# Sampled values of the fifth query group: twelve block transfers from SP's queue in place of four gathers from GpSimd

## The chip, the cores and the metric

The kernel runs on one core of a Trainium2 chip. The metric is the device time of one execution in microseconds (us). The core's engines run side by side and wait for each other by semaphores: PE (TensorE) multiplies and transposes, DVE (VectorE), ACT (ScalarE) and POOL (GpSimd) work on tiles, and SP (SyncE) only issues transfers. SP issues a transfer by itself, in the order of its queue. A gather by a list of rows is issued on POOL, as an instruction between POOL's other work.

## The reference, cut to what matters

```python
# attention: batch 4, 8 heads, 768 positions, head width 64; blocks of 32 positions
scores = scale * np.matmul(q, k.transpose(0, 1, 3, 2))
mask = np.abs(blk_i - blk_j) <= 1                      # the window of three blocks
mask = mask | (blk_i == 0) | (blk_j == 0) | (blk_i == n_blocks - 1) | (blk_j == n_blocks - 1)
for qb in range(n_blocks):
    for kb in sampled_blocks[qb]:                      # three sampled blocks for each query block
        mask[qb * block:(qb + 1) * block, kb * block:(kb + 1) * block] = True
attn = softmax(np.where(mask, scores, -1e9))           # then out = attn @ v
# mixture of experts on the 3072 rows of 512: each token goes to one of 8 experts, 384 tokens each,
# by the descending order of all logits x @ w_gate
for e in range(E):
    mask = assigned == e
    out[mask] = np.maximum(x[mask] @ w1[e], 0.0) @ w2[e]
```

## The kernel before, in words

**Two stages.** `Attn` computes the attention of the four batches one after the other, writes its rows to HBM (`xrows`) and the gate's logits to a tile (`lg`). `Moe` then orders the tokens expert by expert, gathers 384 rows for each expert, multiplies them with weights that were split in two halves, and scatters the results to the output.

**Attention.** A batch's 24 query blocks of 32 positions make one dense part (the first and the last block, kind `D`) and six groups `u` of four blocks each (the sixth, `u` = 5, has two). A query block of a group sees eight key blocks. Four stand in the tile `kg` ahead of the sampled ones (the window of three, and the first or last block), and in the value tile `vw`; the three sampled blocks and the last block stand in the value tile `vz`. `kg` and `vw` have two buffers (`u % 2`), `vz` has three (`u % 3`). For each pair of halves PE multiplies keys and queries (L482), DVE subtracts the row's extreme (L524, L529), PE transposes (L550), ACT takes the exponential (L556), and PE multiplies with the values of `vw` and of `vz` in turn (L577, the value products).

**The sampled values.** `values` writes a batch's value rows with a one behind each head's 64 values (520 words a row, 2080 bytes) to HBM, `vrows`, one tensor for each batch. `group_values` then fills `vz[32 * r : 32 * r + 32, g]` for each query block g and sampled block r, in one of two ways. Where `u` is odd, SP reads the block numbers of the group into registers (L393) and issues a transfer of 32 rows for each block, three for each query block (L397). Where `u` is even, POOL issues one gather of 96 rows for each query block, by the list `vidx` (L401).

**What sets the order.** The instructions of the attention are tasks of a planner (`Plan`). Each task has a place in time, engines on which it may run with a duration for each, and what it needs; the planner takes the tasks one by one, gives copies that may run on either of two engines to the one that ends earlier by its numbers, and writes the instructions out in the order that comes of it. A gather counts 1.22 us of POOL, three transfers 1.6 us of SP. What changes in one task may so move others. The order of `Moe` is made by another clock (`Clock`), which starts at zero and knows nothing of the attention.

**The end.** In the last expert the results leave in three parts j. Ahead of each scatter POOL writes a one-word spacer, and ahead of the first of the three it also issues a transfer `words` of 34 separate words of each of 128 partitions, from a constant tile to a tile that nothing reads.

Of the kernel before, what the change touches and what calls it, by code (L numbers as in the profile page):

```python
# [7 lines left out]
F32 = mybir.dt.float32  # L8
# [167 lines left out]


NG = 2


class Attn:
# [151 lines left out]
    def group_keys(self, b, u, n):  # L333
# [9 lines left out]
        def add(eng, fn):  # L343
            t = pl.add(n, eng, fn, deps=ev + [self.base], after=ts[:1], take=[s] if first[0] else [],
                       use=[s, self.Tslot[b]["k"]], row="kg" if first[0] else None)
            first[0] = False
            ts.append(t)
        any_ = lambda p, a: dict(POOL=p, ACT=a)
        if u < 2:
            for o, t in ((96, 0), (224, S - BS)):  # L350
                def f(e, o=o, t=t):
                    self.copy(e, kg()[:, :, :, o:o + BS], kT()[:, :, None, t:t + BS].to_broadcast([128, HP, 4, BS]))
                add(any_(.6, .7), f)

        for g in range(0, len(self.blocks(u)), NG):
            def f(e, g=g):
                k = kT()
                a = [list(d) for d in k.ap]
                src = bass.AP(tensor=k.tensor, offset=k.offset + 128 * u + BS * g, ap=a[:2] + [[BS, NG], [1, 96]])
                self.copy(e, kg()[:, :, g:g + NG, 0:96], src)  # L360
            add(any_(.4 + NG * .32, .16 + NG * .33), f)

# [12 lines left out]
    def group_values(self, b, u, n):  # L375

        nc, pl = self.nc, self.plan
        vw, vz, vn = self.vw[u % 2], self.vz[u % 3], self.vn[b % 2].rearrange("p c h d -> p c (h d)")
        sw, sz, sn = pl.slot("vw"), pl.slot("vz"), self.vnslot[b]
        self.vslot[b, u] = [sw, sz]  # L380
        ld, bl, tw, tz = self.vld[b], self.blocks(u), [], []

        def aw(eng, fn, need=(), move=0.0, late=0.0):
            tw.append(pl.add(n + late, eng, fn, deps=[ld[c] for c in need] + [self.base], after=tw[:1],
                             take=[] if tw else [sw], use=[sw, sn], move=move, row=None if tw else "vw"))

        def az(eng, fn, deps, move=0.0, late=0.0):
            tz.append(pl.add(n + late, eng, fn, deps=deps, after=tz[:1], take=[] if tz else [sz], use=[sz, sn], move=move, row=None if tz else "vz"))
        both = lambda p, a: dict(POOL=p, ACT=a)
        for g in range(len(bl)) if u % 2 else ():  # L390
            def f(g=g):
                if u not in self.kept:
                    self.kept[u] = nc.values_load_multi_w_load_instructions(  # L393
                        self.tz[0:1, bl[0]:bl[-1] + 1].rearrange("p n r -> p (n r)"), engines=[ET.SP], min_val=0, max_val=NB,
                        skip_runtime_bounds_check_because="the table is clamped on the chip")[1]
                for r in range(3):
                    nc.sync.dma_start(vz[32 * r:32 * r + 32, g], self.vs[b][bass.ds(self.kept[u][3 * g + r] * BS, BS)])  # L397
            az(("SP", 1.6 if b or g else 3.2), f, self.rel[b] + [self.idx], move=0.75, late=0.1 * g)
        for g in range(len(bl)) if u % 2 == 0 else ():
            def f(g=g):  # L400
                nc.gpsimd.indirect_dma_start(out=vz[0:96, g], out_offset=None, in_=self.vs[b],  # L401
                                             in_offset=bass.IndirectOffsetOnAxis(ap=self.vidx[:, bl[g]:bl[g] + 1], axis=0))
            az(("POOL", 1.22), f, self.rel[b] + [self.idx], move=0.8, late=0.1 * g)
        if u < 3:
            def f():
                nc.sync.dma_start(vz[96:128], vn[96:128, 5:6].to_broadcast([32, 4, VR]))
            az(("SP", 0.5), f, [ld[5]], move=0.75)
        if u < 2:
            def f():
                nc.sync.dma_start(vw[96:128], vn[0:32, 0:1].to_broadcast([32, 4, VR]))  # L410
            aw(("SP", 0.5), f, [0], move=0.75)
        for g in range(len(bl)):
            c = [(bl[g] + i) // 4 for i in (-1, 0, 1)]
            q = [32 * ((bl[g] + i) % 4) for i in (-1, 0, 1)]
            at = [(i, 1) for i in range(3)]
            if g == 0 and u:
                at = [(0, 3)]
            elif g == 2:
                at = [(0, 2), (2, 1)]
            for i, w in at:  # L420
                if bl[g] + i - 1 in (0, NB - 1):
                    def f(g=g, i=i):
                        nc.gpsimd.memset(vw[32 * i:32 * i + 32, g], 0.0)
                    aw(("POOL", 0.53), f)
                    continue

                def f(e, g=g, i=i, w=w, c=c[i], q=q[i]):
                    self.copy(e, vw[32 * i:32 * (i + w), g], vn[q:q + 32 * w, c])
                aw(both(.62, .64), f, [c[i]])
        self.vt[b, u] = tw + tz  # L430
# [389 lines left out]
class Moe:  # L820
# [349 lines left out]
    def ffn(self, k):  # L1170
        nc = self.nc
        xh, xl = self.x[k]
        hh = self.xp.tile([128, 8, CAP], F32R, name="hh", bufs=1)
        hl = self.xp.tile([128, 8, CAP], F32R, name="hl", bufs=1)
        lows, ps = [], {}

        def first(f, passes):
            wh, wl = self.weights(8 * k + f // 2)
            o = 128 * (f % 2)
            if 0 in passes:  # L1180
                ps[f] = self.acc()
            for n in passes:
                a, b = ((wh, xh), (wl, xh), (wh, xl))[n]
                for d in range(4):
                    if n == 2:
                        self.force(self.xlow[k][d])
                    self.P.matmul(ps[f], a[:, 256 * d + o:256 * d + o + 128], b[:, d],
                                  start=n == 0 and d == 0, stop=n == 2 and d == 3)
                    yield

        def relu(f):
            self.A.activation(hh[:, f], ps[f], AF.Relu)
            lows.append(self.add(self.low(hl[:, f], ps[f], hh[:, f], OP.max), "DVE", [hh[:, f]], LOW))
            self.open.append(lows[-1])
            if f % 2:
                self.conv(8 * k + f // 2 + LEAD + (2 if k == E - 1 else 0))

        if k == 0:
            yield from first(0, (0, 1))
            yield from first(1, (0, 1))  # L1200
        for f in range(8):
            yield from first(f, (2,) if k == 0 and f < 2 else (0, 1, 2))
            relu(f)
        po = [self.p1.tile([128, DM], F32, name=f"po{j}") for j in range(3)]
        self.second[k] = True

        def product(f, j):
            wh, wl = self.weights(8 * k + 4 + f // 2)
            o = 512 * (f % 2)
            for n, (a, b) in enumerate(((hh, wh), (hl, wh), (hh, wl))):  # L1210
                self.P.matmul(po[j], a[:, f, 128 * j:128 * j + 128], b[:, o:o + 512], start=f == 0 and n == 0,
                              stop=f == 7 and n == 2)
                yield

        def leave(j):
            ot = self.xp.tile([128, DM], F32, name="ot", bufs=4)
            if k == E - 1 and j == 2:
                self.A.activation(ot[:, 0:256], po[j][:, 0:256], AF.Copy)
                self.V.tensor_copy(ot[:, 256:512], po[j][:, 256:512])
            else:  # L1220
                self.A.activation(ot, po[j], AF.Copy)
            self.G.memset(self.spacer, 0.0)
            if k == E - 1 and j == 0:
                words = self.st.tile([128, 34, 2], F32, name="words")
                self.G.dma_start(words[:, :, 0], self.c["places"][:, 0:34])
            s = self.G.indirect_dma_start(out=self.out, out_offset=bass.IndirectOffsetOnAxis(
                ap=self.idx[k][:, j:j + 1], axis=0), in_=ot, in_offset=None)
            for q in self.scat:
                self.tc.declare_no_dep(s.ins, q.ins, reason="every token is in one expert's rows")
            self.scat.append(s)  # L1230

        for j in range(3) if k == E - 1 else (None,):
            for f in range(8):
                self.force(lows[f])
                for i in range(3) if j is None else (j,):
                    yield from product(f, i)
                if f % 2:
                    self.conv(8 * k + 4 + f // 2 + LEAD)
            for i in range(3) if j is None else (j,):
                leave(i)  # L1240
# [229 lines left out]
```

## Time and profile before

| | us |
|---|---|
| median of three runs | 655.55 |
| the three runs | 648.19, 655.55, 659.25 |
| the profiled execution | 656.38 |
| its span, first to last instruction | 654.6 |
| attention in it, until PE's last product of the logits | about 307 |
| ordering of the tokens until the first expert's products | about 307 to 348 |
| experts, and the last scatter's landing | about 348 to 654.6 |

The profile is of one execution. Busy times are sums over one engine's instructions; an engine's idle time is put down to what ended it, and "issue" is idle time for which the profile shows nothing that was waited for. "Remote" is an end of a wait for which it shows no instruction either.

### The profile page before, as it was taken

How to read it: one execution, taken by the hardware profiler on the slowest of the kernel's cores; microseconds unless marked ns; L12 is line 12 of the kernel's file. 1: busy time of each engine (PE TensorE's matmuls, PEld its weight loads, DVE VectorE, ACT ScalarE, POOL GpSimd, SP SyncE). 2: the span in 40 equal slices, each digit the busy share in tenths (PEclk: the TensorE clock that was granted, in tenths of full speed). 3: DMA queues.
4: the chain of work that ended last, by engine and by line, in shares of the span. 5: the costliest groups of instructions: out<-in, count | busy, mean ns of one | idle time of the engine just before them, and what ended most of it. 6: DMA issues, size and time to landing. Idle time of an engine off the chain costs nothing. (4 is left out here: it accounts for less than half of the span.)

```text
span 654.6 us, 20117 instructions
## 1 busy us (share of the span) xinstructions
PE 569.0 (87%) x7403; PEld 449.1 (69%) x7403; DVE 417.9 (64%) x1624; ACT 378.9 (58%) x845; POOL 408.3 (62%) x738
## 2 busy tenths in 40 slices
PE   5788788889889889987139999999999999999996
PEld 3456566567667666665037769687887878889895
DVE  3658567758757757956777868778787886423020
ACT  3847495657757657745436566575756666436230
POOL 5686657467656696651028566775766777777671
PEclk9899898889989989989559999999999999999999
DMA  8998889976497955231035260816444453645311
GB/s 187 255 209 197 216 229 216 229 208 160 120 199 200 249 148 149 92 101 43 1 114 192 90 238 28 282 74 209 146 161 145 148 176 110 216 162 165 137 2 48
DMA packets 125666, 102.27 MB, mean 156 GB/s; under 512 B 81280, under 2 KB 99840, under 8 KB 125568
## 3 DMA queue, kind: packets, MB, share of 16 engines
q1 hardware_dynamic: 117696, 78.44, 44.2%
q0 software_dynamic: 7008, 22.19, 11.4%
q8 instruction: 58, 0.95, 0.6%
q10 hardware_dynamic: 864, 0.36, 0.2%
q14 instruction: 40, 0.33, 0.2%
HBM read 76.38 MB, written 19.24 MB: 146 GB/s over the span
## 5 line engine op out<-in xcount | busy, mean ns | idle before, releaser
L816 POOL TENSOR_TENSOR wlo<-raw,whi 128x512 fp32r<-128x512 f32 x128 | 161.7, 1289 | 55.8 <-ACT whi L816 55.3
L370 POOL COPY kg<-kT 128x128 f32 x264 | 63.6, 289 | 30.8 <-issue 24.3
L272 ACT ACTIVATE vw<-vn 32x520 f32<-32x520 f32 (+2 forms) x108 | 68.6, 635 | 24.5 <-PE ps L577 22.1
L276 POOL COPY vw<-vn 32x520 f32<-32x520 f32 (+2 forms) x88 | 54.0, 614 | 44.5 <-PE ps L577 23.0
L816 PE MATMUL po<-whi,hl 128*128 128x512 f32 x192 | 77.9, 406 | 0.0
L816 PE MATMUL po<-wlo,hh 128*128 128x512 f32 x192 | 77.3, 403 | 0.0
L816 PE MATMUL po<-whi,hh 128*128 128x512 f32 x192 | 76.4, 398 | 0.0
L816 ACT ACTIVATE whi<-raw 128x512 fp32r<-128x512 f32 x128 | 74.2, 621 | 2.3 <-DMA raw<-in_moe_w_dram 2.2
L556 ACT ACTIVATE aT<-ps 128x512 f32<-128x512 f32 x88 | 49.7, 598 | 27.2 <-PE ps L550 10.6
L524 DVE TENSOR_REDUCE mn<-ps 128x2 f32<-128x512 f32 x88 | 56.8, 683 | 11.9 <-PE ps L482 6.0
L816 DVE SCALAR_TENSOR_TENSOR hl<-ph,hh 128x384 fp32r<-128x384 f32 x64 | 35.3, 553 | 40.2 <-ACT hh L816 38.6
L577 PE MATMUL ps<-vz,aT 128*32 128x65 f32 x1408 | 52.3, 232 | 9.7 <-issue 9.7
L529 DVE TENSOR_TENSOR s<-ps,mn 128x512 f32<-128x512 f32 x88 | 58.0, 682 | 3.7 <-PE ps L550 2.8
L577 PE MATMUL ps<-vw,aT 128*32 128x65 f32 x1408 | 53.2, 234 | 8.1 <-issue 7.3
L482 PE MATMUL ps<-kg,qT 64*32 64x256 f32 x1408 | 57.0, 407 | 3.3 <-issue 1.7
L816 PE MATMUL ph<-xhi,whi 128*128 128x384 f32 x256 | 58.6, 345 | 0.9 <-ACT xhi L816 0.9
L816 PE MATMUL ph<-xlo,whi 128*128 128x384 f32 x256 | 57.9, 344 | 0.0
L816 PE MATMUL ph<-xhi,wlo 128*128 128x384 f32 x256 | 57.6, 342 | 0.0
L816 ACT ACTIVATE hh<-ph 128x384 fp32r<-128x384 f32 x64 | 31.0, 485 | 40.6 <-PE ph L816 38.6
L550 PE MATMUL ps<-ident,s 128*128 128x128 f32 x352 | 50.5, 282 | 4.3 <-ACT aT L556 1.6
L401 POOL DMA_INDIRECT vz<-vrows,vidx x48 | 44.8, 933 | 12.9 <-issue 10.7
L577 PEld LDWEIGHTS ps<-vw,aT 128*32 128x32 f32 x1408 | 38.7, 117 | 19.0 <-issue 12.8
(236 smaller groups left out, 1235.8 us busy)
## 6 DMA issues: line engine op xcount, KB each, us to landing
raw<-in_moe_w_dram SPq DMA_DIRECT2D x64, 512.0 KB
vz<-vrows SPq DMA_DIRECT2D x120, 65.0 KB
vrows<-vn SPq DMA_DIRECT2D x12, 520.0 KB
st<-in_k_dram SPq DMA_DIRECT2D x24, 256.0 KB
st<-in_q_dram SPq DMA_DIRECT2D x24, 256.0 KB
vn<-in_v_dram SPq DMA_DIRECT2D x24, 256.0 KB
xrows<-xt SPq DMA_DIRECT2D x20, 256.0 KB
vz<-vn SPq DMA_DIRECT2D x12, 260.0 KB
```

What stands on the lines that cost most here:

```text
L272: nc.scalar.activation(o, i, AF.Copy, scale=scale)
L276: nc.gpsimd.tensor_copy(o, i)
L370: nc.gpsimd.tensor_copy(kg()[:, :, g, 128 + 32 * r:160 + 32 * r], kT()[:, :, bass.ds(pv[3 * g + r] * BS, BS)])
L401: nc.gpsimd.indirect_dma_start(out=vz[0:96, g], out_offset=None, in_=self.vs[b], in_offset=bass.IndirectOffsetOnAxis(ap=self.vidx[:, bl[g] ...
L482: nc.tensor.matmul(x["S"][0][32 * g:32 * g + 32, 256 * j:256 * j + 256], qT[h, p, BS * bl[gi]:BS * bl[gi] + BS], kg[h, p, gi], start=True, ...
L524: nc.vector.tensor_reduce(x["mn"][:, 0:2], x["S"][0].rearrange("p (j y) -> p j y", j=2), axis=AX.X, op=OP.min)
L529: nc.vector.tensor_tensor(x["s"].rearrange("p (j t) y -> p j (t y)", j=2), x["S"][0].rearrange("p (j y) -> p j y", j=2), x["mn"][:, 0:2, N ...
L550: nc.tensor.transpose(ps[:, c - c0], x["s"][:, c], self.ident)
L556: nc.scalar.activation(x["aT"][:, c0:c1], x["ps", c0][:, 0:c1 - c0], AF.Exp, scale=-1.0 if w == 4 else 1.0)
L577: nc.tensor.matmul(av[32 * g:32 * g + 32, 2 * j + s], aT[:, 2 * j + t, 32 * g:32 * g + 32], v[:, gi, h], start=t == 0, stop=t == 1)
L816: return f(*args, **kw)
```

## The change

Two numbers change. The even groups 0 and 2 still gather; group 4 now goes the odd groups' way. The transfer `words` takes 48 words of each partition in place of 34.

```diff
+LISTS = (0, 2)
...
-        for g in range(len(bl)) if u % 2 else ():
+        for g in range(len(bl)) if u not in LISTS else ():
             def f(g=g):
                 if u not in self.kept:
                     self.kept[u] = nc.values_load_multi_w_load_instructions(
...
                 for r in range(3):
                     nc.sync.dma_start(vz[32 * r:32 * r + 32, g], self.vs[b][bass.ds(self.kept[u][3 * g + r] * BS, BS)])
             az(("SP", 1.6 if b or g else 3.2), f, self.rel[b] + [self.idx], move=0.75, late=0.1 * g)
-        for g in range(len(bl)) if u % 2 == 0 else ():
+        for g in range(len(bl)) if u in LISTS else ():
             def f(g=g):
                 nc.gpsimd.indirect_dma_start(out=vz[0:96, g], out_offset=None, in_=self.vs[b],
...
             if k == E - 1 and j == 0:
-                words = self.st.tile([128, 34, 2], F32, name="words")
-                self.G.dma_start(words[:, :, 0], self.c["places"][:, 0:34])
+                words = self.st.tile([128, 48, 2], F32, name="words")
+                self.G.dma_start(words[:, :, 0], self.c["places"][:, 0:48])
```

Over the four batches 16 gathers go and 48 transfers come, with one more read of block numbers into SP's registers, in batch 0. The planner writes another order for all engines of the attention from batch 0's fifth group on; the order from the experts on is the same as before, but for `words`. Lines of the changed kernel are one higher from L179 on.

On POOL, in batch 0, the four gathers of group 4 stand between the copies of group 3's window values and the sampled keys of group 5. In the rows, `vz_107` is `vz[1]`, `vrows_68` and `vn_109` belong to batch 0, `vw_105` is `vw[1]`, `kg_102` and `kg_103` are the two key buffers, and an ISA row sets a register. Before:

```order
L370 COPY kg_102<-kT 128x4x32
L276 COPY vw_105<-vn_109 32x520 x5
L401 DMA vz_107<-vrows_68,vidx 96x520 x4
L365 TENSOR_LOAD tbl
L370 ISA
L370 COPY kg_103<-kT 128x4x32
```

and now:

```order
L371 COPY kg_102<-kT 128x4x32
L277 COPY vw_105<-vn_109 32x520 x5
L366 TENSOR_LOAD tbl
L371 ISA
L371 COPY kg_103<-kT 128x4x32
```

The gathers are gone from between, and the sampled keys of group 5 follow the copies at once.

On SP, in batch 0, the loads of batch 1 (keys and queries to `st`) and the first rows of the output (`xrows`) followed group 3's twelve transfers to `vz_106`. Before:

```order
L397 DMA vz_106<-vrows_68 32x520
L294 DMA st<-in_k_dram 128x8x64
L628 DMA xrows<-xt 128x512
L294 DMA st<-in_q_dram 128x8x64
L628 DMA xrows<-xt 128x512
L294 DMA st<-in_q_dram 128x8x64
L328 DMA vrows_69<-vn_110 128x2x520
L393 TENSOR_LOAD tz
L397 ISA
L397 DMA vz_108<-vrows_68 32x520
```

Now group 4's block numbers and its twelve transfers to `vz_107` come behind the key load:

```order
L398 DMA vz_106<-vrows_68 32x520
L295 DMA st<-in_k_dram 128x8x64
L394 TENSOR_LOAD tz
L398 ISA
L398 DMA vz_107<-vrows_68 32x520
```

and behind the last of the twelve stands what followed the key load before, up to group 5's transfers to `vz_108`:

```order
L398 DMA vz_107<-vrows_68 32x520
L329 DMA vrows_69<-vn_110 128x2x520
L629 DMA xrows<-xt 128x512
L295 DMA st<-in_q_dram 128x8x64 x2
L394 TENSOR_LOAD tz
L398 ISA
L398 DMA vz_108<-vrows_68 32x520
```

Batch 1's value rows, an output row, two query loads and group 5's transfers now stand behind twelve more transfers on SP's queue.

## Rows read from the trace of the kernel before

**Rows 1.** The page, busy time of each engine over the whole span.

```profile
PE 569.0 (87%) x7403; PEld 449.1 (69%) x7403; DVE 417.9 (64%) x1624; ACT 378.9 (58%) x845; POOL 408.3 (62%) x738
```

**Rows 2.** Windows: the attention from 25 to 300 us; the first line names the columns.

```profile
core 0: us, PE busy (x) PEld busy (x) DVE busy (x) ACT busy (x) POOL busy (x), PEclk, DMA share, GB/s
25.00:300.00 275.00, 239.43 (x5494) 176.66 (x5490) 190.94 (x449) 176.02 (x333) 179.25 (x487) 0.95 0.73 183
```

**Rows 3.** Windows: group 4's gathers, four of five windows, and the sum.

```profile
64.30:70.00 5.70, 2.35 (x59) 1.31 (x42) 1.87 (x4) 0.00 (x0) 4.74 (x9) 0.97 1.07 224
136.40:142.10 5.70, 3.33 (x58) 2.67 (x58) 1.83 (x3) 1.13 (x3) 4.74 (x9) 0.94 0.92 276
...
214.00:218.40 4.40, 2.77 (x66) 1.49 (x64) 2.08 (x4) 0.57 (x1) 3.13 (x5) 1.00 1.03 286
278.50:284.30 5.80, 3.07 (x60) 2.26 (x59) 1.19 (x4) 1.27 (x3) 3.71 (x4) 1.00 0.49 135
sum 22.60, PE 12.52 PEld 8.57 DVE 7.94 ACT 3.89 POOL 17.25; mean PE 2.50 PEld 1.71 DVE 1.59 ACT 0.78 POOL 3.45
```

**Rows 4.** Windows: the sum over the eleven windows of groups 0 and 2's gathers.

```profile
sum 46.60, PE 32.35 PEld 20.98 DVE 23.43 ACT 19.71 POOL 36.69; mean PE 2.94 PEld 1.91 DVE 2.13 ACT 1.79 POOL 3.34
```

**Rows 5.** Windows: bursts of SP's transfers to vz without gathers; two of seven, their sum.

```profile
81.90:88.50 6.60, 6.33 (x208) 5.66 (x196) 4.66 (x13) 6.46 (x13) 2.83 (x6) 1.00 0.66 189
128.10:133.50 5.40, 5.40 (x176) 3.98 (x168) 4.74 (x12) 4.12 (x9) 2.47 (x11) 1.00 0.65 204
...
sum 37.40, PE 35.74 PEld 25.89 DVE 32.28 ACT 34.14 POOL 24.10; mean PE 5.11 PEld 3.70 DVE 4.61 ACT 4.88 POOL 3.44
```

**Rows 6.** Timeline of POOL, one gather; waits from 25 to 303 us (total, times, longest).

```profile
65.55 0.92 POOL L401 DMA_INDIRECT vz<-vrows,vidx  x1 [0.30 <-issue]
...
POOL vw L276 <- DMA vz<-vrows,vidx: 12.5, 5, 3.8
```

**Rows 7.** Timeline of PE in batch 0's window: two of five stalls.

```profile
66.30 0.27 PE L577 MATMUL ps<-vz,aT 128*32 128x65 f32 x2 [0.39 <-issue]
...
69.90 0.27 PE L577 MATMUL ps<-vw,aT 128*32 128x65 f32 x1 [1.16 <-issue]
```

**Rows 8.** Waits from 64 to 70.5 us: total, times, longest.

```profile
ACT lp L272 <- remote: 6.2, 1, 6.2
...
DVE mn L524 <- remote: 3.8, 2, 3.2
```

**Rows 9.** Windows at the low clock, and the value products' mean there and at 84 us.

```profile
69.70:73.10 3.40, 3.20 (x111) 3.18 (x113) 0.69 (x1) 1.15 (x3) 0.71 (x4) 0.50 0.74 189
...
sum 13.60, PE 12.78 PEld 11.32 DVE 4.46 ACT 5.69 POOL 3.40; mean PE 4.26 PEld 3.77 DVE 1.49 ACT 1.90 POOL 1.13
...
L577 PE MATMUL ps<-vw,aT 128*32 128x65 f32 x50 | 3.0, 314 | 1.2 <-issue 1.2
...
L577 PE MATMUL ps<-vw,aT 128*32 128x65 f32 x64 | 2.0, 222 | 0.0
```

**Rows 10.** SP's queue: timeline of batch 0, and one wait between 136 and 156 us.

```profile
66.48 8.31 SPq L397 DMA_DIRECT2D vz<-vrows  x12
...
78.10 1.14 SPq L328 DMA_DIRECT2D vrows<-vn  x1
81.96 2.11 SPq L397 DMA_DIRECT2D vz<-vrows  x3
...
SPq L294 <- PE ps L302: 6.7, 1, 6.7
```

**Rows 11.** Timeline of POOL at the end; the window while `words` is moved.

```profile
632.07 1.83 POOL L816 DMA_DIRECT2D words<-c_places  x1
639.44 1.01 POOL L816 DMA_INDIRECT out_dram<-ot,idx  x1 [5.54 <-ACT ot L816]
...
646.18 0.98 POOL L816 DMA_INDIRECT out_dram<-ot,idx  x1 [5.65 <-issue]
...
634.00:640.00 6.00, 6.00 (x28) 4.93 (x27) 0.16 (x1) 0.60 (x1) 0.56 (x1) 1.00 0.38 3
```

## The prediction, as it was written before the result

> **What bounds the kernel now.** I began with the page [rows 1]: PE is busy for 87% of the span, and no other engine for more than 64%. That is an average over two stages. The change touches the order of the attention alone, and the `words` at the end; the experts' order is the same before and after. So I asked the windows for the attention by itself [rows 2]: from 25 to 300 us PE is busy for 239.4 of 275 us, the others for 176 to 191. PE is the bound there, and 35.6 us of it are idle. What matters is when these 35.6 us come and what ends them.
>
> The list of waits says "issue" for most of it: PE sat still in the middle of a run of value products, with nothing in the profile that it waited for [rows 7]. In batch 0 there are five such stalls between 65 and 70 us, and that is when POOL runs group 4's four gathers. The other engines stand too: ACT waits 6.2 us and DVE 3.8 us for something that the profile does not show [rows 8]. So I put windows over all gathers. In the five windows of group 4 (in batch 2 its first gather stands apart, in a window of 1 us that is not shown) PE is busy for 12.5 of 22.6 us [rows 3]; DVE and ACT, at 7.9 and 3.9 us, do no more. In the eleven windows of groups 0 and 2 it is 32.4 of 46.6 us [rows 4]. Both together are 24.3 of the 35.6 idle us, in a quarter of the time.
>
> The counter-test is the same kind of value products while SP's block transfers are issued and no gather is: over seven bursts PE is busy for 35.7 of 37.4 us, and for all of 5.4 us in one of them [rows 5]. Traffic is not what divides the two: the DMA share is 0.49 in the last of group 4's windows, where PE is idle for 2.7 of 5.8 us, and 0.65 and 0.66 in the two bursts shown. So in this trace a gather on POOL goes with a standing PE, and SP's transfers do not. The cause I cannot name; that the gather is the cause is an inference from sixteen windows against seven.
>
> **The change, part by part.**
>
> *Stalls of PE.* Group 4's windows hold 22.60 - 12.52 = 10.1 us of idle PE [rows 3]. Without gathers 1.66 of 37.4 us would be usual [rows 5], 4.4%, which is 1.0 us of 22.6. So 9.1 us come back if the gathers cause the stalls, and none if they do not. Between 0 and -10.1 us I take -9.1, since the bursts of rows 5 are the very thing that replaces the gathers.
>
> *The clock.* After three of the four shown PE ran at a granted clock of 0.50, the lower of its two levels (1.2 GHz): for 3.4, 6.8 and 3.4 us, each from about the end of a stall on [rows 9]. In these 13.6 us PE was busy for 12.78. If all of that ran at the full clock, half of it would be saved, 6.4 us. The rows' own durations say less: a value product took 314 ns there and 222 ns at 84 us, a third less, 12.78 x (1 - 222/314) = 3.7 us. If the fall comes from elsewhere it is 0. Between 0 and -6.4 I take -3.7, the value from the durations.
>
> *POOL.* 16 gathers of 0.92 us with 0.30 us behind each [rows 6] are 19.5 us less on POOL. POOL is busy for 179 of 275 us [rows 2], so that by itself is worth nothing: it lies beside PE's work. Copies of window values waited five times, 12.5 us in total and at most 3.8, for gathers issued ahead of them [rows 6]. One such wait with a cover that fails could be worth as much as its longest, so 0 to -3.8; I take 0, since value products were not late for the window values. What the planner moves with it (copies change sides between ACT, POOL and DVE) I also take at 0: these engines have some 84 to 99 us of idle time each in the stretch [rows 2].
>
> The Trainium skill speaks against the change here: the page "DMA: Bandwidth & Descriptors", section "Issuing engines are not separate DMA queues", says that transfers from SP, ACT and GpSimd run on the same 16 DMA engines, and that another issuing engine saves only the sequencer's issue time. By that rule alone the saving would be POOL's 19.5 us, none of it on the path, and the sum would be no change. The windows above do not agree with it as far as PE is concerned; the rule's outcome is the first rival.
>
> *SP's queue.* Twelve transfers took SP 8.31 us in batch 0 [rows 10]. They now stand ahead of batch 1's query loads and of group 5's transfers. Before, SP sat idle there from 79.2 (78.10 + 1.14) to 81.96 us, 2.7 us [rows 10], so in batch 0 what follows comes at most 8.3 - 2.7 = 5.6 us later. In batch 1 SP stood 6.7 us in one wait for PE to free a load buffer [rows 10], which covers most of the burst; batch 3 has no next batch to load. The queue is also where PE's gain is spent: group 4's own values must land before its products, and PE will come to them some 5 us sooner in batch 0. Bounds: 0, if the slack hides all, and +5.6 for batch 0 alone (without any slack in three batches 25 us, a rival below). A gain is excluded: SP gets only more. I take +2, nearer the lower end, for the one place without enough slack.
>
> *The `words`.* 48 for 34 words make 1.83 us of POOL into 2.6 at the same rate, from 632.07 to 634.7; the scatter behind it starts at 639.44, when the result is ready [rows 11]. The words' own traffic takes part of 634 to 640 us (DMA share 0.38) while PE is busy throughout [rows 11]. Cost 0, covered by the last expert's products; without this cover +0.8.
>
> By the section "The descriptor swizzle" of the same page of the Trainium skill, a 128-partition transfer has for each DMA engine eight data descriptors and one for its completion. An estimate from that page: a gather of 96 rows takes 6 + 1, sixteen gathers 112, and 14 more words on 128 partitions also 112, so the last three scatters would stand where they stood in POOL's queue. No run here shows it, and the sum does not use it.
>
> The sum against the profiled execution: 656.4 - 9.1 - 3.7 + 2.0 = 645.6 us. The profiled execution lies 0.8 us above the median of 655.55, so the same for a median is 644.8. I predict **645 us**, 1.6% below.
>
> **The rivals.**
>
> *The stalls stay (no change).* The place could be at fault and not the gather: a long run of short products, with much going on beside. Then the same standing follows the transfers, or moves to groups 0 and 2. For it: the cause is unnamed, and stalls between groups 0 and 2 differ widely with the place. Against it: seven bursts without stalls [rows 5]. Time: 656, from 651 to 659 with the runs' own spread.
>
> *SP's queue takes over (slower).* Values of groups 3, 4 and 5 now all come from one queue that issues in order, with the next batch's keys and queries between. If SP has no slack, three batches lose 8.3 us each in late query loads and late values: 656.4 + 25 - 12.8 = 668. It decides where PE's transposes of loaded queries (L302) or the products of groups 4 and 5 start to wait for transfers. For it: batch 0's queue is full but for 2.7 us. Against it: 6.7 us of waiting in batch 1, and SP waits for PE and not the reverse.
>
> *More than forecast.* All stalls go (10.1), the whole low clock (6.4) and a late copy (3.8), and SP costs nothing: 656.4 - 20.3 = 636. For it: POOL gets freer in the stage where PE is the bound. Against it: groups 0 and 2 still gather and still lower the clock.
>
> The change does do what it says: the instructions stand in the order.
>
> **How the numbers follow.** Forecast, 639 to 651: 0.52. Stalls stay, 651 to 659: 0.25. More, under 639: 0.14. SP takes over, above 659: 0.09. The range is 636 to 657: it reaches down to the full gain and up over most of the no-change case, and leaves out about 2 in 10. A measurement of this kernel can tell about 2% from no change, 642.4 and 668.7 us here. Below 642.4 lie the third rival and about a third of the forecast's own spread: 0.32. Above 668.7 lies less than half of the slower case: 0.04. The rest is 0.64.
>
> **What would show it.** Right: in the changed profile's attention PE loses its "issue" stalls in three or four places per run where group 4's value transfers are issued, the low clock appears fewer times, SP shows bursts of twelve transfers twice in a row in batches 0 and 3, the ordering of the tokens starts about 10 us earlier than at 307, and the time from there to the end is the same. Wrong: PE idle in those places as before, or waits of PE for `vz` or `st` transfers, or the remaining 32 gathers covering more value products than now, which the new order decides and which I cannot read from the trace.

## The result, and the profile after

The changed kernel takes 659.59 us (median of four runs, 657.16 to 662.10) against 652.07 us for the kernel before (four runs, 648.19 to 659.25): ratio 1.0132, 95% interval 1.0087 to 1.0177. It is 1.3% slower; 645 us were predicted, with a range to 657. The group's part of the change alone measured 1.0113 on another chip (e5, below), so the sign doesn't hang on one chip.

The profiled execution took 661.24 us, with a span of 659.4 us. Busy time on its page, to be set beside [rows 1]:

```profile
PE 564.9 (86%) x7403; PEld 444.2 (67%) x7403; DVE 412.3 (63%) x1612; ACT 381.3 (58%) x848; POOL 397.6 (60%) x731
```

The windows say in which stage the time went. The first row answers to [rows 2], the second is a part of it:

```profile
25.00:300.00 275.00, 230.50 (x5352) 166.92 (x5348) 182.03 (x428) 176.80 (x330) 166.41 (x477) 0.95 0.75 182
75.00:100.00 25.00, 11.57 (x208) 9.20 (x210) 6.66 (x20) 8.76 (x19) 8.95 (x30) 0.80 0.76 197
```

The second row before:

```profile
75.00:100.00 25.00, 21.07 (x507) 15.84 (x506) 18.77 (x58) 21.57 (x41) 15.23 (x102) 1.00 0.88 233
```

PE is busy for 230.5 of 275 us, 8.9 less than before, and between 75 and 100 us for 11.6 of 25, with every other engine below 10; before, it was busy for 21.1 of these 25. In the waits of PE (25 to 310 us: total, times, longest) a new name leads, `xt`, the buffer of output rows:

```profile
PE ps L652 <- DVE xt L620: 8.6, 1, 8.6
PE ps L483 <- POOL kg L371: 5.2, 3, 2.7
PE ps L578 <- issue: 5.0, 4, 2.2
PE ps L483 <- issue: 4.8, 3, 2.5
PE ps L303 <- DMA st<-in_k_dram: 3.5, 2, 2.0
PE ps L681 <- DVE xt L620: 3.4, 2, 2.9
PE ps L551 <- DVE xt L620: 2.7, 1, 2.7
```

The "issue" waits of the value products are 5.0 us in 4 stalls. In the profile before they led the list:

```profile
PE ps L577 <- issue: 17.0, 29, 1.2
```

That looks like what was predicted, but it is not shown to be the change's doing: e1 and e9 below, which have all gathers in the order of the kernel before, show 4 and 6 such stalls too. Behind `xt` stands DVE, and behind DVE a store, as DVE's timeline and its waits show:

```profile
87.76 0.42 DVE L620 TENSOR_TENSOR xt<-ps,rc 128x256 f32<-128x256 f32 x1 [9.01 <-DMA xrows<-xt]
...
DVE xt L620 <- DMA xrows<-xt: 29.7, 6, 9.0
```

The store frees one of the two `xt` buffers. Where it was is in SP's timeline of batch 0, which answers to [rows 10]:

```profile
65.50 8.02 SPq L398 DMA_DIRECT2D vz<-vrows  x12
73.63 0.40 SPq L295 DMA_DIRECT2D st<-in_k_dram  x1
76.73 6.74 SPq L398 DMA_DIRECT2D vz<-vrows  x12
83.52 0.42 SPq L329 DMA_DIRECT2D vrows<-vn  x1
84.03 0.41 SPq L629 DMA_DIRECT2D xrows<-xt  x1
84.53 1.74 SPq L295 DMA_DIRECT2D st<-in_q_dram  x2
```

Read from above: group 3's twelve transfers, one load of keys, group 4's twelve, and only then the store and two loads of queries. The same store before:

```profile
75.38 0.53 SPq L628 DMA_DIRECT2D xrows<-xt  x1
```

It is issued at 84.03 us in place of 75.38. DVE stands 9.01 us for the store, PE 8.6 us for DVE, and the granted clock falls to 0.50, its lower level, from 83.2 to 93.4 us.

The end of the program is as it was. POOL's timeline of the `words` and the last three scatters answers to [rows 11]:

```profile
636.93 2.30 POOL L817 DMA_DIRECT2D words<-c_places  x1
644.30 1.02 POOL L817 DMA_INDIRECT out_dram<-ot,idx  x1 [5.07 <-ACT ot L817]
650.86 0.98 POOL L817 DMA_INDIRECT out_dram<-ot,idx  x1 [5.45 <-issue]
655.47 0.97 POOL L817 DMA_INDIRECT out_dram<-ot,idx  x1 [3.54 <-DVE ot L817]
```

The first read of rows for an expert (POOL's timeline, first of the kernel before, then of the changed one) splits the run in two:

```profile
340.35 1.00 POOL L816 DMA_INDIRECT xg<-xrows,row  x1 [6.34 <-DVE pk L816]
```

```profile
344.73 1.00 POOL L817 DMA_INDIRECT xg<-xrows,row  x1 [6.33 <-DVE pk L817]
```

From there to the end of the span it is 314.3 us before and 314.7 us after. All but 0.4 of the 4.8 us between the two spans were lost ahead of the experts.

### The profile page after: what moved, and what is told of

It reads as the page before. It is cut to its first block, busy times and chain, and to the rows that moved or that the text cites. A ratio compares the mean times of both kernels' runs of the same rounds, so it can differ in the third digit from the quotient of the medians.

```text
span 659.4 us, 20221 instructions
## 1 busy us (share of the span) xinstructions
PE 564.9 (86%) x7403; PEld 444.2 (67%) x7403; DVE 412.3 (63%) x1612; ACT 381.3 (58%) x848; POOL 397.6 (60%) x731
## 5 line engine op out<-in xcount | busy, mean ns | idle before, releaser
L277 POOL COPY vw<-vn 32x520 f32<-32x520 f32 (+2 forms) x97 | 59.5, 614 | 42.8 <-DMA vz<-vrows,vidx 16.3
L273 ACT ACTIVATE vw<-vn 32x520 f32<-32x520 f32 (+2 forms) x99 | 62.8, 635 | 19.2 <-PE ps L578 17.0
L483 PE MATMUL ps<-kg,qT 64*32 64x256 f32 x1408 | 61.0, 396 | 11.9 <-POOL kg L371 5.2
L483 PEld LDWEIGHTS ps<-kg,qT 64*32 64x32 f32 x1408 | 26.9, 109 | 35.8 <-POOL kg L371 13.8
L578 PE MATMUL ps<-vw,aT 128*32 128x65 f32 x1408 | 45.8, 226 | 4.3 <-issue 3.8
L551 PEld LDWEIGHTS ps<-ident,s 128*128 128x128 f32 x352 | 40.8, 147 | 10.8 <-DVE xt L620 2.8
L578 PE MATMUL ps<-vz,aT 128*32 128x65 f32 x1408 | 46.7, 224 | 1.6 <-issue 1.1
```

The costliest lines, as they stand in the source:

```text
L273: nc.scalar.activation(o, i, AF.Copy, scale=scale)
L277: nc.gpsimd.tensor_copy(o, i)
L483: nc.tensor.matmul(x["S"][0][32 * g:32 * g + 32, 256 * j:256 * j + 256], qT[h, p, BS * bl[gi]:BS * bl[gi] + BS], kg[h, p, gi], start=True, ...
L551: nc.tensor.transpose(ps[:, c - c0], x["s"][:, c], self.ident)
L578: nc.tensor.matmul(av[32 * g:32 * g + 32, 2 * j + s], aT[:, 2 * j + t, 32 * g:32 * g + 32], v[:, gi, h], start=t == 0, stop=t == 1)
```

## The experiments

My first theory (A) was the rows above taken literally: the two `xt` buffers are too few while a store stands behind twelve transfers; without that wait the predicted gain appears. The rival (C): the planner's other order as such. e1 to e4, e5 to e8, e9 to e12, e13 to e16, and e17 and e18 ran together, each group on a chip of its own. Ratios are to the kernel before on that chip; times are compared within a group only.

Some edits leave the order of the instructions alone, as the traces show: e1, e6, e9 and e14 keep the order of the kernel before (e16 too, but for two stores), e3 to e5, e13 and e15 that of the changed kernel (in e4 the stores go from SP to ACT). In e2, e7, e8, e10 to e12, e17 and e18 the planner wrote another order for all engines, so their times hold also what moved with the edit.

**e1, the words alone.** In the changed kernel:

```diff
-LISTS = (0, 2)
+LISTS = (0, 2, 4)
```

> Group 4 gathers as before; only the 48 words are new. Theory A (the loss is all in the attention, by stores of output rows that stand on SP's queue behind group 4's transfers): as before, ratio 0.998 to 1.003, attention end at 307 us, the words' DMA 2.3 us instead of 1.83 with its cover. Rival B (the longer words push the scatters of the last expert): ratio 1.004 or more, and the stretch from the attention's end to the end of the span grows by 2 us or more.

Measured: 648.73 us, ratio 0.9903 [0.9867, 0.9938], five runs. Neither theory: faster, though the order of the attention is word for word that of the kernel before. e9 and e6 come back to it.

**e2, batch 0 by gathers.**

```diff
-        for g in range(len(bl)) if u not in LISTS else ():
+        for g in range(len(bl)) if not (u in LISTS or (u == 4 and b == 0)) else ():
...
-        for g in range(len(bl)) if u in LISTS else ():
+        for g in range(len(bl)) if u in LISTS or (u == 4 and b == 0) else ():
```

> The changed kernel with batch 0's group 4 sampled by gathers again; batches 1 to 3 by SP's transfers. Theory A: the stand of 8.55 us at 79 to 88 us goes, and with it 2 to 3 us of low clock behind it, so 646 to 651 us, ratio 0.990 to 1.000 against before. Rival C (the loss is the planner's new order as such, spread over POOL's copies of keys, window values and loads): the loss stays in the other three batches, 656 us or more, ratio 1.007 or more.

Measured: 653.51 us, 1.001 [0.9967, 1.0053]. With batch 0 as before, the loss is gone, but the other three batches gain nothing; the order of all engines moved too.

**e3, a third `xt` buffer, and e4, the stores by ACT.**

```diff
...
-                state["x"] = (wk.tile([128, H, D], F32, name="xt") if kind == "I"
+                state["x"] = (wk.tile([128, H, D], F32, name="xt", bufs=3) if kind == "I"
```

```diff
-                nc.sync.dma_start(self.xd[r0 + 128 * u:r0 + 128 + 128 * u], state["x"].rearrange("p h d -> p (h d)"))
+                nc.scalar.dma_start(self.xd[r0 + 128 * u:r0 + 128 + 128 * u], state["x"].rearrange("p h d -> p (h d)"))
```

> The changed kernel, order of every engine unchanged, with a third buffer for the output rows (xt), for which some tables of the start are put into a key buffer that is not in use yet. DVE then waits for the store before the last but one. Theory A: most of PE's 15.7 us of waits for DVE's xt go, less what turns up behind it, and the clock stays up there: 645 to 651 us, ratio 0.990 to 0.999. Rival C: what stands behind the xt waits are other late things (loads of keys and queries on the same queue, copies on POOL), so PE waits as long for those: 656 to 660 us, ratio 1.007 or more.

> The changed kernel, order unchanged but for the stores of the output rows, which ACT issues at the place where SP did. They no longer stand behind group 4's transfers, but each waits on ACT for DVE's last xt. Theory A: xt is freed early, PE's stand of 8.55 us goes; ACT pays 20 issues and some waits for DVE: 645 to 653 us, ratio 0.990 to 1.003. Rival C: 656 us or more.

Measured: e3 661.56 us, 1.0119 [1.0071, 1.0168]; e4 671.08 us, 1.0257 [1.0219, 1.0296]. Theory A falls. The waits of PE in e3:

```profile
PE ps L303 <- DMA st<-in_q_dram: 15.0, 5, 8.4
PE ps L483 <- POOL kg L371: 11.9, 2, 7.7
PE ps L578 <- issue: 3.7, 2, 3.3
```

and the stand of batch 0 in its timeline of PE:

```profile
88.31 1.98 PE L303 MATMUL ps<-ident,st 128*128 128x128 f32 x7 [8.38 <-DMA st<-in_q_dram]
```

The wait for `xt` is gone, and PE stands 8.4 us at the same place for the load of queries, which stood behind the same twelve transfers. In e4 it is 8.8 us for such a load. One wait had hidden the other. So theory D: it is SP's queue as a whole that is late. e4 is slower still than e3, with longer waits of PE for loads of keys (5.0 us, 0.7 in e3) and for POOL's copies of keys (15.5 and 11.9); why was not tried.

**e5, the group alone (34 words), and e6, the kernel before with the wider tile.**

```diff
-                words = self.st.tile([128, 48, 2], F32, name="words")
-                self.G.dma_start(words[:, :, 0], self.c["places"][:, 0:48])
+                words = self.st.tile([128, 34, 2], F32, name="words")
+                self.G.dma_start(words[:, :, 0], self.c["places"][:, 0:34])
```

```diff
-                words = self.st.tile([128, 34, 2], F32, name="words")
+                words = self.st.tile([128, 48, 2], F32, name="words")[:, 0:34]
```

> Group 4 by SP's transfers as in the changed kernel, with the 34 words of the kernel before. If the words are worth the 1% by which they alone measured faster, and the two edits add up: 662 to 666 us, ratio 1.016 to 1.025. If the words do nothing and that 1% was the spread of the attention from run to run: as the changed kernel, ratio 1.009 to 1.017.

> The kernel before with a tile for 48 words of which 34 are loaded: the experts' buffers move by 96 bytes in a partition, POOL's queue carries what it carried. If the words' 1% came from the buffers' places: 647 to 650 us, ratio 0.988 to 0.994. If it came from what POOL's queue carries, or from chance: ratio 0.996 to 1.004.

Measured: e5 669.27 us, 1.0113 [1.0054, 1.0173]; e6 662.80 us, 0.9999 [0.9956, 1.0042]. The group carries the whole loss, and the buffers' places do nothing.

**e7, group 4's transfers later.**

```diff
-                self.group_values(b, u, at[u] - 7.5)
+                self.group_values(b, u, at[u] - (7.5 if u != 4 else 7.5 - 5))
```

> The changed kernel with group 4's transfers due 5 planner units later, so that in batches 0 and 1 a store of output rows or a load of queries stands between every three to six of them. Theory D (it is SP's queue as a whole that is late in batch 0: output rows, and behind them query loads, stand behind twelve transfers in a row): the stand at 79 to 88 us shrinks to 3 us or less: 646 to 653 us, ratio 0.989 to 1.000. Rival C (the planner's new order as such, or POOL's copies of keys): 656 us or more, ratio 1.005 or more.

Measured: 658.62 us, 0.9936 [0.9901, 0.9970]; 10.7 us less than e5 beside it, which has 34 words. Where the transfers stand in SP's order, with all that the planner moved along, is worth 1.6%.

**e8, group 3 by gathers too.**

```diff
-LISTS = (0, 2)
+LISTS = (0, 2, 3, 4)
```

> The opposite change: groups 0, 2, 3 and 4 by gathers (16 more than before, 48 fewer transfers of SP), with 48 words. If gathers make PE stand, as the prediction's first term has it (10 us of stalls for 16 gathers, and the low clock behind them): 658 us or more, ratio 1.005 or more against before. If they don't, and it is SP's queue that costs: 640 to 650 us, ratio 0.980 to 0.995.

Measured: 683.48 us, 1.0280 [1.0188, 1.0372]. The 16 more gathers and the order around them cost 20.2 us between the medians, although 48 transfers are gone from SP: more than the prediction's first two terms have for 16.

**e9, the words alone once more.**

> The same kernel as the words alone, beside the kernel before on another chip, and beside the three kernels below. If the longer words load makes the attention faster: ratio 0.986 to 0.995 again. If the first ratio was the spread of the attention between loads of a program or between chips: 0.996 to 1.004. Its trace also shows the order of the kernel before on the chip of the next three.

Measured: 651.91 us, 0.9999 [0.9964, 1.0035], ten runs. The words are worth nothing; the interval of e1 did not cover the spread between chips.

**e10, SP's transfers beside the gathers.** In the kernel before, group 4 keeps its gathers, and SP copies the blocks aside:

```diff
...
+                for r in range(3):
+                    o = 32 * (12 * b + 3 * g + r)
+                    nc.sync.dma_start(self.vs[B][o:o + 32], self.vs[b][bass.ds(self.kept[u][3 * g + r] * BS, BS)])
+            pl.add(n + 0.1 * g, ("SP", 1.6 if b or g else 3.2), f, deps=self.rel[b] + [self.idx], move=0.75)
...
```

> The kernel before with all its gathers, and beside them the transfers that the change would add: group 4's 48 blocks of every batch are copied by SP into a DRAM tensor that nothing reads (nine of batch 0's twelve stand ahead of the output rows and the query load, as in the changed kernel). Theory D (SP's queue is what costs, and the gathers that go away give little): 1.010 to 1.022, as the changed kernel or somewhat more. If the loss came from the values of group 4 themselves landing late, or from the copies that moved to other engines: 0.996 to 1.007.

Measured: 659.97 us, 1.0115 [1.0046, 1.0183]. The transfers and the order around them cost this even where nobody reads what they bring. The waits of PE show what is late, loads and stores of SP's queue:

```profile
PE ps L302 <- DMA st<-in_q_dram: 13.5, 6, 6.1
PE ps L302 <- DVE xt L629: 9.4, 1, 9.4
```

Two things e10 does not hold apart: the place in SP's queue, and the traffic that the transfers add (from 25 to 300 us the DMA share is 0.78 here and 0.74 in e9).

**e11, group 4's values not loaded, and e12, e7 with 34 words.** e11 is the kernel before with group 4 out of the loop of gathers and nothing in its place:

```diff
-        for g in range(len(bl)) if u % 2 == 0 else ():
+        for g in range(len(bl)) if u in (0, 2) else ():
...
+        if u == 4:
+            az(("DVE", 0.01), lambda: None, self.rel[b] + [self.idx])
```

> Group 4's sampled values are not loaded at all, by neither way (its products read what the buffer held), 34 words: the gathers of group 4 go and nothing takes their place. The prediction's first two terms (stalls of PE and the low clock that the gathers bring, 12.8 us): 0.976 to 0.986. If PE stands as long without these gathers: 0.994 to 1.004.

> Group 4's transfers due 5 planner units later, with the 34 words of the kernel before: the best version so far without the words. If it is SP's burst in batch 0 that costs and the words do nothing: 0.989 to 0.998, as with 48 words. If the words carried that gain: 1.000 or more.

Measured: e11 640.46 us, 0.9814 [0.9742, 0.9887], 12.1 us of 652.11; e12 654.31 us, 1.0023 [0.9992, 1.0054]. Without group 4's gathers, in a new order, nearly the 12.8 us come back that the prediction had for them. By its ratio e12 beats the changed kernel, but not the kernel before. Its own expectation reads 1.000 or more as the words' doing; e9 on the same chip gives the words nothing, so e7's gain was not repeated, and e18 asks for it once more.

**e13 to e16, transfers, gathers and order apart.** e13 leaves out all of group 4's transfers and e15 those of batch 0, both in the changed kernel's order; e14 leaves out group 4's gathers in the order of the kernel before; e16 is the kernel before with the change in batch 3 only. The reads of block numbers that go with the transfers are not shown:

```diff
 e13
...
-                for r in range(3):
+                for r in range(3 if u != 4 else 0):
 e15
...
-                for r in range(3):
+                for r in range(0 if u == 4 and b == 0 else 3):
 e14
             def f(g=g):
+                if u == 4:
+                    return
                 nc.gpsimd.indirect_dma_start(out=vz[0:96, g], out_offset=None, in_=self.vs[b],
 e16
-        for g in range(len(bl)) if u % 2 else ():
+        for g in range(len(bl)) if not (u in LISTS or (u == 4 and b < 3)) else ():
...
-        for g in range(len(bl)) if u % 2 == 0 else ():
+        for g in range(len(bl)) if u in LISTS or (u == 4 and b < 3) else ():
```

> The order of the changed kernel, word for word, with group 4's 48 transfers and their register loads left out (its products read what the buffer held). Theory D (the transfers' time in SP's queue is the price): 0.975 to 0.990. Rival C (the order that the planner writes is the price): 1.003 or more.

> The order of the kernel before, word for word, with group 4's 16 gathers left out (its products read what the buffer held). If the gathers cost what the run without group 4 gained, by POOL's copies that wait for them and by stalls of PE: 0.975 to 0.988, PE's waits for POOL's copies of keys 0 to 4 us instead of 13.5. If that gain was the other order: 0.994 to 1.002.

> The order of the changed kernel with batch 0's twelve transfers of group 4 left out, the other 36 in place. If batch 0's burst is the price (PE stands 8.6 us at 79 us for it): 0.993 to 1.002. If all batches pay alike: 1.005 to 1.010. If the order is the price: 1.010 or more.

> The kernel before with group 4 by SP's transfers in batch 3 only, 34 words; nothing else in the order moves but two stores of output rows. There is no next batch whose loads would stand behind them. If SP's transfers are free there, as the prediction has it for this batch, a quarter of the gathers' 12 us comes back: 0.993 to 0.998. If not: 0.999 to 1.005.

Measured, beside 650.62 us of the kernel before: e13 642.11 us, 0.9887 [0.9846, 0.9928]; e14 639.49 us, 0.9829 [0.9787, 0.9871]; e15 652.88 us, 1.0023 [0.9988, 1.0058]; e16 649.95 us, 0.9980 [0.9942, 1.0019], which decides nothing. e13 speaks against rival C: the changed kernel's order without the transfers is faster than before. It lacks the gathers too; beside e14, which lacks them in the old order, the new order costs 2.6 us between the medians, within the noise of the two. e15 lies at the upper edge of its first range: batch 0's twelve transfers are part of the price, not all of it.

What batch 0's twelve did shows in e15's timeline of SP, where they are gone from the same order:

```profile
72.87 0.42 SPq L629 DMA_DIRECT2D xrows<-xt  x1
```

The store that the changed kernel issues at 84.03 us is issued here at 72.87, and PE's longest wait between 70 and 95 us is 1.5 us in place of 8.6.

For the 36 transfers of the other batches the path is less clear. In e15 DVE waits for stores for 15.1 us, in e13 for 4.4:

```profile
DVE xt L620 <- DMA xrows<-xt: 15.1, 5, 5.1
...
PE ps L483 <- POOL kg L371: 16.9, 3, 11.1
```

But PE's own waits for `xt` and for loads of `st` come to no more than 3.9 us in e15, and its longest one, 11.1 us, is for POOL's copies of keys (16.9 us in all, 10.6 in e13). Slower landing is a rival that no run holds apart: a store of `xrows` takes 4.8 us from issue to landing (median) in the changed kernel and 3.5 us in e14, a load of queries 5.7 and 4.4 us.

How the gathers cost is seen by laying e14 beside e9, which has the order of the kernel before. POOL's and PE's waits from 25 to 310 us, first e9:

```profile
POOL vw L277 <- DMA vz<-vrows,vidx: 32.4, 8, 7.0
...
PE ps L483 <- POOL kg L371: 13.5, 4, 7.3
PE ps L578 <- issue: 8.0, 6, 2.3
```

then e14:

```profile
POOL vw L276 <- DMA vz<-vrows,vidx: 15.6, 4, 6.4
...
PE ps L579 <- issue: 6.7, 5, 2.8
PE ps L484 <- POOL kg L370: 2.7, 1, 2.7
```

Copies of window values on POOL wait until gathers have landed; the copies of keys stand behind them on POOL, and PE's products of queries and keys wait for those. PE's "issue" stalls in value products are 1.3 us apart, its waits for keys 10.8 us. The two are of different chips; e11, on e9's chip but in its new order, has 1.5 us of waits for keys. The wait for the gathers is in the program: ahead of such copies POOL's queue holds semaphore instructions of the copies' line (36 of L277 in e9) that wait for the gathers' semaphores, though the copies do not read what the gathers bring. Why the program has them, and what it costs to be without, was not tried.

**e17, the window copies off POOL, and e18, e7 again.** In the kernel before:

```diff
-                aw(both(.62, .64), f, [c[i]])
+                aw(dict(DVE=.62, ACT=.64), f, [c[i]])
```

> The kernel before (all its gathers, 34 words) with the copies of window values by ACT or DVE only, never by POOL. If the gathers cost through POOL's copies that wait for them to land (32 us of such waits, 13.5 us of PE behind POOL's copies of keys): these waits vanish, PE waits for POOL's keys 0 to 5 us, ratio 0.985 to 0.995. If ACT and DVE pay for the 40 to 80 copies with what PE wins: 0.997 to 1.010, with PE's waits for ACT's aT and DVE's s in its place.

> The kernel with group 4's transfers due 5 units later and 48 words, once more on another chip and in five rounds. If it beats the kernel before: ratio 0.990 to 0.997 again. If the first ratio was the spread between chips: 0.998 to 1.005, as with 34 words.

Measured, beside 651.73 us: e17 645.87 us, 0.9882 [0.9843, 0.9920]; e18 649.12 us, 0.9964 [0.9926, 1.0002]. e17 keeps all 48 gathers and is faster than both kernels, by the ratios. Windows of its attention, with POOL 42.4 us less busy than in [rows 2] and DVE 25.3 us more:

```profile
25.00:300.00 275.00, 238.84 (x5652) 176.22 (x5651) 216.21 (x520) 190.20 (x359) 136.88 (x402) 0.96 0.74 184
```

No wait of PE for `kg` is left in it. That fits the path through POOL's copies, but as the order of all engines is new in e17, its gain is not shown to come from that alone. For e18 the interval touches 1: with e7 and e12 the later placing gives 0.994, 1.002 and 0.996, at most a small gain over the kernel before.

## Why the prediction was wrong

**The step that failed** is the term of SP's queue, +2 with bounds 0 and +5.6: it measured +16. The terms by experiment, each from its own ratio and the kernel before beside it: gathers gone in the old order -11.1 us (e14); the planner's new order 0.9887 - 0.9829, +3.8 us; the 36 transfers of batches 1 to 3 1.0023 - 0.9887, +8.9 us (e15 against e13); batch 0's twelve 1.0132 - 1.0023, +7.1 us (the changed kernel against e15). They add up to the result, +7.5 between the medians and +8.6 by the ratio, because each is the step from one kernel to the next; that sum is no test of them. Each carries 3 to 4 us of uncertainty, so the order's +3.8, which the prediction put at 0, is hardly clear of nothing, and the last compares two chips (with e5's 1.0113 in place of 1.0132 it would be +5.9).

**Stalls and clock**, -9.1 and -3.7: right in size (12.8 predicted; 11.1 in e14, 12.1 in e11), but by luck, as on the chips of these two runs the path was another. The prediction read the "issue" stalls of one profile [rows 3, 7] as what gathers cost, and put POOL's copies at 0 [rows 6]. In e9 and e14 the cost goes through these copies. On the chip of e5 to e8 the "issue" stalls are there; the waits of PE for the same program as before but for the tile, e6,

```profile
PE ps L577 <- issue: 15.8, 24, 1.3
```

and with 16 gathers fewer, in e5, are nearly alike:

```profile
PE ps L578 <- issue: 16.1, 21, 2.4
```

All lines of PE's waits that say "issue" come to 26.7 us (39 times) in e6 and 20.2 us (29) in e5, and to 14.1 us (11) in e9 and 12.1 us (9) in e14. So 16 gathers go with 6.5 us of such stalls on one chip and 2.0 on the others, by one profile each, not with 9.1.

On that one chip the inference from sixteen windows against seven holds as far as place goes. Of e6's 39 "issue" waits 23 overlap a gather on POOL, though the gathers take 45 of the 285 us; in e5 it is 19 of 29, with 30 us of gathers; in the profile before, 29 of 40. In e9, with the same order as e6, it is 3 of 11. The step that was not sound is from one profile to the kernel on any chip. Nor does the number of stalls in value products follow the number of gathers there: 20 and 21 with 32 gathers (e7, e5), 24 with 48 (e6), 21 with 64 (e8). How much of the 11.1 us is the clock was not measured apart.

**POOL, 19.5 us at no gain**: wrong. The bound of -3.8 us was the longest wait for a gather, taken as if one wait only could matter. In e9 there are eight such waits, 32.4 us, and PE waits 13.5 us for copies of keys that stand behind them.

**SP's queue.** The prediction counted slack: 2.7 us of idle SP in batch 0, a wait of 6.7 us in batch 1. It counted it for loads of queries and for the values, not for the stores of output rows, whose landing frees `xt`. The 2.7 us (79.2 to 81.96) also lie behind the store and the loads of queries, so they could cover nothing for these: the store moved by 8.6 us, from 75.38 to 84.03, not by at most 5.6. And it took SP's waiting in batch 1 as cover, where e15 against e13 shows that batches 1 to 3 pay 8.9 us; by which path stays open.

**The rival** "SP's queue takes over" had the mechanism, shown for batch 0, and a price that was too high: 668 us, with 25 us for three batches, where 16 were measured for four. Its point of decision named the loads (L302), which is where PE stands once `xt` is out of the way (e3); the wait seen first was L652's. It had a chance of 0.09.

The Trainium skill's page "DMA: Bandwidth & Descriptors", section "Issuing engines are not separate DMA queues", had spoken for no change. The measured +1.3% is not that; its rule says nothing of two things that counted here, what stands behind a transfer on the queue of the engine that issues it (the store, 8.6 us later) and what waits on POOL for a gather (32.4 us in e9).

**The words**, 0: right (e9 0.9999; e6, with the wider tile alone, 0.9999). The load took 2.30 us, 2.6 were predicted. The estimate that 14 words make up for 16 gathers in POOL's queue is borne out: the middle one of the last three scatters waits for "issue" in the kernel before and in the changed one (5.65 and 5.45 us), and with 48 words beside 48 gathers, in e9, it does not:

```profile
643.31 0.98 POOL L817 DMA_INDIRECT out_dram<-ot,idx  x1 [4.39 <-ACT ot L817]
```

Over all twenty profiles the wait stands in the eleven with 48 gathers and 34 words or 32 gathers and 48 words, and in none of the nine with other pairs. The count of descriptors from the Trainium skill's page "DMA: Bandwidth & Descriptors", section "The descriptor swizzle", by which the two pairs come out equal, agrees with that. The wait is worth nothing at the end: the last scatter starts 0.74 us after ACT's last copy in all three.

## What to carry to other kernels

Before work is moved to a queue that issues in order, write down everything that stands behind the new place, stores too, and for each the buffer that it frees and who waits for that; idle time of the queue covers only what stands behind it, and taking one wait away may only show the one hidden behind it. What a removed operation costs is best measured by leaving it out with the order kept (e14), and the price of its replacement by leaving that out (e13): the two together said what no wait in the profile before did. Where the "issue" stalls were few, the dear part of the gathers was what waited for them on POOL; the kernel with these copies off POOL, in a new order, gained 1.2% with all gathers in place. And a profile of one execution on one chip may show a path that other chips do not have.

## What was not expected of the hardware

- The kernel before takes 663.27 us on the chip of e5 to e8 and 650.6 to 653.6 us on four others. On the first the value products of all four kernels show 20 to 24 "issue" stalls, most of them short (29 in the profile before); in the profiles of all other runs there are 2 to 8. With the order of instructions the same, e6 and e9 lose about as much by PE's waits (39.7 and 44.0 us in all, from 25 to 310 us): e6 in stalls, most of them beside gathers, e9 in waits for POOL. What makes a chip one or the other stays open.
- A ratio of 0.9903 with an interval of 0.9867 to 0.9938 (e1) came out as 0.9999 on another chip (e9): such an interval does not cover what another chip changes, here about 1%.
- The experts can give back part of what the attention gains. Their first read of rows comes at 339.18 us in e9 and at 321.41 in e14, 17.8 us earlier, and the spans end 12.9 us apart (653.0 and 640.1). Why was not tried.
